# Row statistics and the scaling of k on GpSimd in a retention, SoLU and cosine-gate kernel

## The chip, the cores and the metric

The kernel runs on one core of one Trainium2 chip. The metric is device time in microseconds (us), the median of several runs. Five engines matter: PE (TensorE matmul; its weight loads have a row of their own, PEld), DVE (VectorE), ACT (ScalarE), POOL (GpSimd) and SP (SyncE, which here only issues DMAs). Each runs its own list of instructions in order: an instruction that waits holds up everything behind it on its engine.

## The reference

Three stages follow each other. Stage 1 is linear attention with decay, for 4 batches, 8 heads, 768 positions and head size 64. Stage 2 is a SoLU block with a normalisation, for 3072 rows. Stage 3 is a block with a cosine gate.

```python
for t in range(S):
    state = gamma * state + einsum('bhd,bhe->bhde', k[:, :, t], v[:, :, t])
    y[:, :, t] = scale * einsum('bhd,bhde->bhe', q[:, :, t], state)
...
h = x @ w_in                       # 3072x512 by 512x1024
sm = exp(h - max(h)); sm = sm / (sum(sm) + 1e-9)
solu = h * sm
ln = (solu - mean(solu)) / sqrt(var(solu) + 1e-6) * g_ln
x = ln @ w_out                     # 1024x512
...
h = x @ w_in                       # 512x2048
return (h * cos(h)) @ w_out        # 2048x512
```

## The kernel before

The work is cut into 24 attention steps of 64 positions for two batches, 24 row blocks of 128 rows for stage 2, and 6 blocks of 512 rows for stage 3. Matmuls keep fp32 accuracy by splitting each factor into a high and a low part (`split`: ACT rounds, DVE subtracts) and multiplying three of the four pairs. The weights arrive as 64-bit floats and are taken apart in `load_w`: one ACT instruction (L158) and four on DVE (L161, L162, L164, L167).

An attention step n has these parts:

- `load_step` issues six DMAs from SP: `kt` (L91), two halves of `X` (q, L93 and L94), two halves of `W` (v, L96 and L97), `kn` (k by rows, L98). The buffers go round: 3 for X, kn and W, 2 for kt and mg.
- `att_prep` multiplies the mask by the step's decay (`mg`, L219, one POOL instruction of 128x512) and scales `kn` by a constant per partition and pair of heads (L223, four ACT instructions of 128x128).
- `score_pair` and `state_pair` are the PE parts (L230, L231 and L241); `score_mask` (DVE, L248) writes the masked scores into X; `state_copy` (ACT, L255 and L256) copies the running state into W of the next step; `att_out` (PE L287, DVE L290) gives the rows x.

Stage 2 of a row block n: `split_x` (L125 on ACT, L128 on DVE), `mm1` (PE L315) in two column halves, then `norm`. `norm` is a chain over ACT, DVE and POOL: DVE takes the maximum (L323), ACT the exponential with its sum (L324), DVE the product with h and its sum (L325); then come the one-column statistics `sm` (128x1): minus the mean (L327, DVE), the square of the deviations (L328, ACT, result `junk`), the sum of exponentials plus 1e-9 (L329, DVE), its square times 1e-6 (L330, DVE), the variance plus that (L332, DVE), the power -1/2 (L334, POOL), and mean times that power (L335, DVE). L336 (ACT) applies scale and bias to `u`. Two row blocks later in program order `transp` transposes u on PE (L351), splits it (`lth` on ACT L354, `ltl` on DVE L355), and `mm2` multiplies (PE L368); its result goes to DRAM through ACT (`ys`, L372). `load_o1` prepares the weights of mm2 (L180 on ACT, L181 on DVE). Weights for stage 3 are unpacked between these steps and parked in DRAM (L191). Stage 3 (`up`, `down`) uses PE L393 and L418 and none of the lines above.

The order on PE is the order of the program, as written by hand at the end of `body`. The other engines' orders are made by the scheduler, which may move an instruction ahead of earlier ones. So `kn` of a step can be scaled, in ACT's order, well before the step itself.

Of the kernel before, what the change touches and what calls it, by code (L numbers as in the profile page):

```python
# [15 lines left out]
AF = mybir.ActivationFunctionType  # L16
ALU = mybir.AluOpType
# [4 lines left out]
B, H, S, D = 4, 8, 768, 64  # L22
# [3 lines left out]
NHP = H // 2  # L26
DM = H * D
FF1 = 1024
# [22 lines left out]
def body(ctx: ExitStack, tc: tile.TileContext, qx, kt, kn, vn, c_sc, c_mg,  # L51
         w_in1, w_out1, gln, w_in2, w_out2, out):
    nc = tc.nc
# [52 lines left out]
    cs = const.tile([128, 3, NI, NHP], F32, name="cs")  # L106
# [109 lines left out]
    def att_prep(n):  # L216
        bp, i = steps[n]
        d = st[n]
        nc.gpsimd.tensor_tensor(out=d["mg"], in0=mg, in1=cs[:, 0:2, i].unsqueeze(3).to_broadcast([128, 2, NHP, C]),  # L219
                                op=ALU.mult)  # L220
        if i + 1 < NI:
            for a in range(NHP):
                nc.scalar.activation(out=d["kn"][:, a], in_=d["kn"][:, a], func=AF.Copy, scale=cs[:, 2, i, a:a + 1])  # L223

    def score_pair(n, j):
        d = st[n]
# [91 lines left out]
    def norm(n):  # L318
        h = hs.pop(n)
        sm = sms[n % 3]  # L320
        junk = moe.tile([128, 2, 512], BF16, tag="junk", name="junk")
        u = p_u.tile([128, 2, 512], F32, tag="u", name="u")
        nc.vector.tensor_reduce(out=sm[:, 0:1], in_=h, axis=AX.XY, op=ALU.max, negate=True)  # L323
        nc.scalar.activation(out=u, in_=h, func=AF.Exp, bias=sm[:, 0:1], accum_out=sm[:, 1:2])  # L324
        nc.vector.scalar_tensor_tensor(out=u, in0=u, scalar=1.0, in1=h, op0=ALU.mult, op1=ALU.mult,  # L325
                                       accum_out=sm[:, 2:3])
        nc.vector.tensor_scalar(out=sm[:, 3:4], in0=sm[:, 2:3], scalar1=-1.0 / FF1, scalar2=None, op0=ALU.mult)  # L327
        nc.scalar.activation(out=junk, in_=u, func=AF.Square, bias=sm[:, 3:4], accum_out=sm[:, 4:5])  # L328
        nc.vector.tensor_scalar(out=sm[:, 5:6], in0=sm[:, 1:2], scalar1=1e-9, scalar2=None, op0=ALU.add)  # L329
        nc.vector.scalar_tensor_tensor(out=sm[:, 6:7], in0=sm[:, 5:6], scalar=1e-6, in1=sm[:, 5:6],  # L330
                                       op0=ALU.mult, op1=ALU.mult)
        nc.vector.scalar_tensor_tensor(out=sm[:, 7:8], in0=sm[:, 4:5], scalar=1.0 / FF1, in1=sm[:, 6:7],  # L332
                                       op0=ALU.mult, op1=ALU.add)
        nc.gpsimd.tensor_tensor(out=sm[:, 8:9], in0=sm[:, 7:8], in1=mhalf, op=ALU.pow)  # L334
        nc.vector.tensor_tensor(out=sm[:, 9:10], in0=sm[:, 3:4], in1=sm[:, 8:9], op=ALU.mult)  # L335
        nc.scalar.activation(out=u, in_=u, func=AF.Identity, scale=sm[:, 8:9], bias=sm[:, 9:10])  # L336
        lns[n] = u

# [118 lines left out]
    def attend():  # L457
        n = nxt[0]
        if n >= ns:
            return  # L460
        nxt[0] += 1
        if 4 < n + 2 < ns:
            load_step(n + 2)
        if n == 0:
            att_state(n)
            att_out(n)
        if n + 1 < ns:
            att_prep(n + 1)
            if n > 0 and "lt" in p2:
                att_both(n)  # L470
            else:
                att_scores(n + 1)
        if n > 0:
            if "lt" not in p2:
                att_state(n)
            att_out(n)
        if n == ns - 1:
            att.close()
            p2["psh"] = ctx.enter_context(tc.tile_pool(name="psh", bufs=3, side="right", space=PSUM, reuse_waits="tile"))
            p2["sb"] = ctx.enter_context(tc.tile_pool(name="sb2", bufs=1, side="right", reuse_waits="tile"))  # L480

    def first(n, c):
        if c == 1 and 0 < n < 2 * NG - 1:
            split_x(n + 1)
        mm1(n, c)
        if c == 1:
            norm(n)
# [5 lines left out]
    load_step(2)  # L493
    fetch_w1(1)
    att_prep(0)
    att_scores(0)
    weights(KD)
    att_state(0)
    att_out(0)
    att_prep(1)  # L500
    att_scores(1)
    split_x(0)
# [164 lines left out]
```

## Time and profile before

| | |
|---|---|
| time, median of 3 runs | 931.45 us (930.01 to 932.88) |
| span of the profiled execution | 932.8 us; no other time of its own is given, and the highest run, 932.88, is nearest |
| PE busy | 893.4 us, 96% |
| PEld busy | 765.1 us, 82% |
| DVE busy | 622.7 us, 67% |
| ACT busy | 455.5 us, 49% |
| POOL busy | 48.0 us, 5%, 60 instructions |
| mean granted TensorE clock | 0.985 of full speed |
| DMA | 85.28 MB, mean 91 GB/s |

Busy time is the time in which an engine executes; shares are of the span. A row with `[... <-X]` or "idle before" says how long the engine stood idle before an instruction, and which instruction, transfer or engine ended that idle time. The chain of waits follows the end of the program back to its start, always to what released each piece. In order listings, `x4` means four such instructions in a row; numbers behind tile names (sm_121) tell buffers of one tile apart.

### The profile page before, as it was taken

To read this page: it belongs to the slowest core of one execution; us is meant where nothing else is said; L and a number is where in the kernel's file an instruction comes from. 1 tells how busy PE (TensorE), PEld (TensorE's weight loads), DVE (VectorE), ACT (ScalarE), POOL (GpSimd) and SP (SyncE) were. 2 spreads that over 40 slices of the span, in tenths; PEclk is the share of its full clock that TensorE was granted. 3 is DMA by queue.
4 is the path that set the end of the run, shared out by engine and by line. 5 is a ranking of instruction groups with operands and counts; after the bars stand their busy time and mean duration, and the time that the engine had idled before them with its cause. 6 is when DMAs were issued, how large, how long until landed. Compare 5 with 4: busy or idle time off the path is not lost.

```text
span 932.8 us, 16044 instructions
## 1 busy us (share of the span) xinstructions
PE 893.4 (96%) x6464; PEld 765.1 (82%) x6464; DVE 622.7 (67%) x1090; ACT 455.5 (49%) x768; POOL 48.0 (5%) x60
## 2 busy tenths in 40 slices
PE   4787999989899999999999999999999999999997
PEld 4676889879799989998888888888888888888886
DVE  6899887587667754566766655756575665656654
ACT  4677666556656555554534333433443343344332
POOL 2112100101011000000000000000000000000000
PEclk7999899989999999999999999999999999999999
DMA  9986354565547422133012002000300030001001
GB/s 260 313 252 194 106 158 146 184 204 161 188 131 226 157 93 90 64 108 111 24 35 56 1 1 73 19 0 1 91 1 1 7 84 1 1 24 45 1 1 46
DMA packets 41884, 85.28 MB, mean 91 GB/s; under 512 B 5457, under 2 KB 11729, under 8 KB 41809
## 3 DMA queue, kind: packets, MB, share of 16 engines
q1 hardware_dynamic: 41376, 83.91, 30.0%
q8 instruction: 51, 0.84, 0.4%
q10 hardware_dynamic: 432, 0.34, 0.1%
q14 instruction: 25, 0.20, 0.1%
HBM read 64.30 MB, written 19.92 MB: 90 GB/s over the span
## 4 chain that ended last, share of the span: by engine, by line
PE 84%; DVE 6%; DMA 5%; ACT 2%; issue 2%; SPq 1%; POOL 0%; DVEq 0%; ACTq 0%
PE h L393 28%; PE acc L418 28%; PE y L368 13%; PE h L315 10%; DMA kn<-kn_dram 3%; PE tr L351 2%; PE y L287 2%; DMA W<-vn_dram 1%; PE sc L230 1%; DVE X L248 1%; DVE wt L164 1%; DVE wt L161 1%; ACT kn L223 1%; ACT junk L328 1%; DVE wt L162 0%
## 5 line engine op out<-in xcount | busy, mean ns | idle before, releaser
L393 PE MATMUL h<-yh,w2h 128*128 128x512 f32 x384 | 149.6, 390 | 0.0
L393 PE MATMUL h<-yl,w2h 128*128 128x512 f32 x384 | 149.4, 389 | 0.0
L393 PE MATMUL h<-yh,w2l 128*128 128x512 f32 x384 | 149.4, 389 | 0.0
L418 PE MATMUL acc<-o2h,gh 128*128 128x512 f32 x384 | 149.4, 389 | 0.0
L418 PE MATMUL acc<-o2h,gl 128*128 128x512 f32 x384 | 149.4, 389 | 0.0
L418 PE MATMUL acc<-o2l,gh 128*128 128x512 f32 x384 | 149.4, 389 | 0.0
L404 ACT ACTIVATE r<-r,hp 128x512 f32<-128x512 f32 x96 | 69.5, 724 | 144.5 <-DVE r L403 144.5
L368 PE MATMUL y<-lth,o1h 128*128 128x256 f32 x384 | 110.2, 287 | 0.0
L368 PE MATMUL y<-ltl,o1h 128*128 128x256 f32 x384 | 108.8, 283 | 0.0
L368 PE MATMUL y<-lth,o1l 128*128 128x256 f32 x384 | 108.6, 283 | 0.0
L401 DVE SCALAR_TENSOR_TENSOR r<-ki,h 128x512 f32<-128x512 int32 x96 | 66.0, 687 | 62.9 <-ACT ki L400 61.9
L405 DVE TENSOR_TENSOR r<-r,h 128x512 f32<-128x512 f32 x96 | 66.0, 687 | 61.6 <-ACT r L404 61.6
L128 DVE TENSOR_TENSOR gl<-r,gh 128x512 fp32r<-128x512 f32 x96 | 66.3, 691 | 45.9 <-ACT gh L125 45.4
L400 ACT ACTIVATE ki<-h 128x512 int32<-128x512 f32 x96 | 57.3, 597 | 74.7 <-PE h L393 74.1
L125 ACT ACTIVATE gh<-r 128x512 fp32r<-128x512 f32 x96 | 60.7, 632 | 65.4 <-DVE r L405 65.4
L393 PEld LDWEIGHTS h<-yh,w2h 128*128 128x128 f32 x384 | 72.1, 188 | 14.9
L418 PEld LDWEIGHTS acc<-o2h,gl 128*128 128x128 f32 x384 | 72.1, 188 | 15.0
L393 PEld LDWEIGHTS h<-yl,w2h 128*128 128x128 f32 x384 | 72.1, 188 | 15.0
L418 PEld LDWEIGHTS acc<-o2l,gh 128*128 128x128 f32 x384 | 72.1, 188 | 14.9
L418 PEld LDWEIGHTS acc<-o2h,gh 128*128 128x128 f32 x384 | 72.0, 188 | 14.9
L393 PEld LDWEIGHTS h<-yh,w2l 128*128 128x128 f32 x384 | 72.1, 188 | 14.8
L315 PE MATMUL h<-w1h,xh 128*128 128x512 f32 x192 | 77.9, 406 | 0.0
(77 smaller groups left out, 1554.3 us busy)
## 6 DMA issues: line engine op xcount, KB each, us to landing
raw<-w_in_dram SPq DMA_DIRECT2D x24, 512.0 KB, 4.4
raw<-w_out_dram SPq DMA_DIRECT2D x24, 512.0 KB, 4.8
kt<-kt_dram SPq DMA_DIRECT2D x24, 256.0 KB, 4.9
X<-qx_dram SPq DMA_DIRECT2D x48, 128.0 KB, 5.0
W<-vn_dram SPq DMA_DIRECT2D x48, 128.0 KB, 4.6
kn<-kn_dram SPq DMA_DIRECT2D x24, 256.0 KB, 5.1
y1d<-ys SPq DMA_DIRECT2D x24, 256.0 KB, 2.1
yt<-y1d SPq DMA_DIRECT2D x24, 256.0 KB, 2.9
```

The source lines that it names most:

```text
L125: op = nc.scalar.activation(out=hi, in_=src if head is None else head, func=AF.Copy)
L128: nc.vector.tensor_tensor(out=lo, in0=src, in1=hi.bitcast(F32), op=ALU.subtract)
L287: nc.tensor.matmul(out=y[64 * par:64 * par + 64, j], lhsT=d["W"][:, par, j], rhs=d["X"][:, par, j], start=True, stop=True)
L315: nc.tensor.matmul(out=h[:, c], lhsT=a[:, k], rhs=w[:, k, cs], start=(k + m == 0), stop=(k == KD - 1 and m == 2))
L351: nc.tensor.transpose(out=tr[:, e, t * 128:(t + 1) * 128], in_=lns[2 * g + t].rearrange("p c f -> p (c f)")[:, j * 128:(j + 1) * 128], ide ...
L368: nc.tensor.matmul(out=y1[:, e], lhsT=w[:, j, ds], rhs=a[:, j % 2], start=(m == 0), stop=(m == 3 * K1 - 1))
L393: nc.tensor.matmul(out=h, lhsT=w[:, k, cs], rhs=a[:, k], start=(m == 0), stop=(m == 3 * KD - 1))
L400: nc.scalar.activation(out=ki, in_=h, func=AF.Identity, scale=INV2PI, bias=0.25)
L401: nc.vector.scalar_tensor_tensor(out=r, in0=ki, scalar=-C1, in1=h, op0=ALU.mult, op1=ALU.add)
L404: nc.scalar.activation(out=r, in_=r, func=AF.Sin, bias=hp[:, 0:1])
L405: nc.vector.tensor_tensor(out=r, in0=r, in1=h, op=ALU.mult)
L418: nc.tensor.matmul(out=acc, lhsT=a[:, ts_], rhs=w, start=(j == 0 and m == 0), stop=(j == K2 - 1 and m == 2))
```

## The change

Two edits. In `att_prep` one POOL instruction over 128x512 scales kn, with the constants broadcast along the 128 columns of a pair of heads, in place of four ACT instructions over 128x128. In `norm` the instructions of L329, L330, L332 and L335 go from DVE to POOL, with forms that POOL has (the factor 1e-3 is applied before squaring, so the square is 1e-6 times as before); L327, minus the mean, stays on DVE.

```diff
@@ att_prep
         if i + 1 < NI:
-            for a in range(NHP):
-                nc.scalar.activation(out=d["kn"][:, a], in_=d["kn"][:, a], func=AF.Copy, scale=cs[:, 2, i, a:a + 1])
+            nc.gpsimd.tensor_tensor(out=d["kn"], in0=d["kn"], in1=cs[:, 2, i].unsqueeze(2).to_broadcast([128, NHP, 2 * D]),
+                                    op=ALU.mult)
@@ norm
-        nc.vector.tensor_scalar(out=sm[:, 5:6], in0=sm[:, 1:2], scalar1=1e-9, scalar2=None, op0=ALU.add)
-        nc.vector.scalar_tensor_tensor(out=sm[:, 6:7], in0=sm[:, 5:6], scalar=1e-6, in1=sm[:, 5:6],
-                                       op0=ALU.mult, op1=ALU.mult)
-        nc.vector.scalar_tensor_tensor(out=sm[:, 7:8], in0=sm[:, 4:5], scalar=1.0 / FF1, in1=sm[:, 6:7],
-                                       op0=ALU.mult, op1=ALU.add)
+        nc.gpsimd.tensor_scalar(out=sm[:, 5:6], in0=sm[:, 1:2], scalar1=1e-9, scalar2=1e-3,
+                                op0=ALU.add, op1=ALU.mult)
+        nc.gpsimd.tensor_tensor(out=sm[:, 6:7], in0=sm[:, 5:6], in1=sm[:, 5:6], op=ALU.mult)
+        nc.gpsimd.tensor_scalar(out=sm[:, 7:8], in0=sm[:, 4:5], scalar1=1.0 / FF1, scalar2=sm[:, 6:7],
+                                op0=ALU.mult, op1=ALU.add)
         nc.gpsimd.tensor_tensor(out=sm[:, 8:9], in0=sm[:, 7:8], in1=mhalf, op=ALU.pow)
-        nc.vector.tensor_tensor(out=sm[:, 9:10], in0=sm[:, 3:4], in1=sm[:, 8:9], op=ALU.mult)
+        nc.gpsimd.tensor_tensor(out=sm[:, 9:10], in0=sm[:, 3:4], in1=sm[:, 8:9], op=ALU.mult)
```

In the changed kernel the square is L331; the other line numbers are as before, but for kn's scaling, which is L222. PE's order is the same instruction for instruction, SP's the same but for a handful of neighbours that change places. Of POOL's 22 new kn instructions and 96 new statistics, the place matters.

ACT, near the start of the program, after the first unpacked weights (`xh` is the split of the first row block). Before, kn of steps 1 and 2 stands ahead of the state copies and of a weight's high part:

```order
L125 ACTIVATE xh<-x_265 128x512
L223 ACTIVATE kn<-kn,cs 128x128 x4
L125 ACTIVATE w1h<-wt 128x512
L223 ACTIVATE kn<-kn,cs 128x128 x4
L255 ACTIVATE W<-S 64x512
L256 ACTIVATE W<-S 64x512
L125 ACTIVATE w1h<-wt 128x512
```

and in the changed kernel:

```order
L125 ACTIVATE xh<-x_262 128x512
L125 ACTIVATE w1h<-wt 128x512 x2
L255 ACTIVATE W<-S 64x512
L256 ACTIVATE W<-S 64x512
```

Both weight parts now follow xh directly.

ACT, at the tenth row block (its statistics are in sm_121), before:

```order
L324 ACTIVATE u,sm_121<-h,sm_121 128x1024
L255 ACTIVATE W<-S 64x512
L256 ACTIVATE W<-S 64x512
L223 ACTIVATE kn<-kn,cs 128x128 x4
L328 ACTIVATE junk,sm_121<-u,sm_121 128x1024
L336 ACTIVATE u<-u,sm_121 128x1024
L158 ACTIVATE wt<-raw 128x512
```

and in the changed kernel:

```order
L324 ACTIVATE u,sm_121<-h,sm_121 128x1024
L255 ACTIVATE W<-S 64x512
L256 ACTIVATE W<-S 64x512
L328 ACTIVATE junk,sm_121<-u,sm_121 128x1024
L336 ACTIVATE u<-u,sm_121 128x1024
L158 ACTIVATE wt<-raw 128x512
```

kn is gone from ahead of junk; u and the unpacking of a weight still stand in the same order behind it.

POOL, at the same tenth row block, as a piece of the difference (- before, + changed):

```order
+L329 TENSOR_SCALAR sm_121<-sm_121 128x1
+L331 TENSOR_TENSOR sm_121<-sm_121 128x1
+L222 TENSOR_TENSOR kn<-kn,cs 128x512
 L219 TENSOR_TENSOR mg<-mg,cs 128x512
+L332 TENSOR_SCALAR sm_121<-sm_121 128x1
 L334 TENSOR_TENSOR sm_121<-sm_121,mhalf 128x1
+L335 TENSOR_TENSOR sm_121<-sm_121 128x1
```

The scaling of kn, and mg behind it, now stand on POOL between the first and the second half of the row block's statistics.

## Rows read from the trace of the kernel before

**Rows 1.** Busy time by stretch: us from:to and length, then each engine, PEclk, DMA
```profile
27.00:41.00 14.00, 9.07 (x113) 7.29 (x112) 13.86 (x25) 8.76 (x19) 2.45 (x2) 0.88 1.06 295
41.00:93.50 52.50, 42.60 (x759) 35.50 (x757) 50.79 (x91) 40.10 (x78) 10.80 (x11) 0.99 0.80 230
93.50:256.00 162.50, 154.80 (x1677) 138.56 (x1678) 120.17 (x239) 99.34 (x175) 18.52 (x20) 0.96 0.53 163
256.00:380.00 124.00, 124.00 (x1172) 113.15 (x1171) 80.41 (x168) 68.77 (x113) 11.13 (x14) 1.00 0.42 133
```

**Rows 2.** Who waited for whom, PE: us in total, times, longest us
```profile
PE tr L351 <- DVE ltl L355: 7.6, 5, 4.1
...
PE tr L351 <- DVE sm L329: 3.8, 1, 3.8
```

**Rows 3.** The chain of waits through the tenth row block: start us, us, what
```profile
173.33 7.86 DMA kn<-kn_dram
...
181.22 1.28 ACT kn L223 x4
182.50 1.14 ACT junk L328 x2
...
183.90 0.56 POOL sm L334
...
184.74 0.04 ACT u L336
...
190.65 0.61 DVE ltl L355
```

**Rows 4.** Groups of ACT instructions, 27 to 93.5 us: count, busy us, mean ns, idle before
```profile
L223 ACT ACTIVATE kn<-kn,cs 128x128 f32<-128x128 f32 x36 | 11.6, 392 | 4.9 <-DMA kn<-kn_dram 4.9
```

**Rows 5.** Groups of POOL instructions, whole program
```profile
L219 POOL TENSOR_TENSOR mg<-mg,cs 128x512 f32<-128x512 f32 x24 | 27.2, 1137 | 210.1 <-DVE x L290 162.0 <-DVE sm L330 45.2 <-DMA cs<-c_sc_dram 2.4
L334 POOL TENSOR_TENSOR sm<-sm,mhalf 128x1 f32<-128x1 f32 x24 | 17.8, 743 | 119.9 <-DVE sm L332 119.9
...
L112 POOL MEMSET mhalf<- 128x1 f32 x1 | 0.1, 93 | 0.0
```

**Rows 6.** DVE and POOL in order of time, 54 to 57 us
```profile
54.15 0.69 DVE L167 SCALAR_TENSOR_TENSOR raw<-raw,wt 128x512 int32<-128x512 int32 x1
...
55.70 1.09 POOL L219 TENSOR_TENSOR mg<-mg,cs 128x512 f32<-128x512 f32 x1 [0.46 <-DVE x L290]
55.81 1.53 DVE L167 SCALAR_TENSOR_TENSOR raw<-raw,wt 128x512 int32<-128x512 int32 x1
```

**Rows 7.** Groups of DVE instructions, 27 to 93.5 us
```profile
L248 DVE TENSOR_TENSOR X<-sc,mg 64x512 f32<-64x512 f32 x18 | 12.3, 684 | 0.2
L167 DVE SCALAR_TENSOR_TENSOR raw<-raw,wt 128x512 int32<-128x512 int32 x11 | 10.1, 919 | 0.1
...
L161 DVE TENSOR_SCALAR wt<-wt 128x512 f32<-128x512 f32 x11 | 6.2, 572 | 0.0
L290 DVE TENSOR_TENSOR x<-y,mg 128x512 f32<-128x512 f32 x9 | 6.2, 689 | 0.2
L162 DVE TENSOR_SCALAR wt<-wt 128x512 int32<-128x512 int32 x11 | 5.3, 497 | 0.0
L325 DVE SCALAR_TENSOR_TENSOR u<-u,h 128x1024 f32<-128x1024 f32 x4 | 4.9, 1218 | 0.1
L323 DVE TENSOR_REDUCE sm<-h 128x1 f32<-128x1024 f32 x4 | 4.9, 1214 | 1.2 <-PE h L315 1.2
...
L335 DVE TENSOR_TENSOR sm<-sm 128x1 f32<-128x1 f32 x3 | 1.3, 432 | 0.0
```

**Rows 8.** DVE in order of time, single instructions
```profile
10.18 0.43 DVE L161 TENSOR_SCALAR wt<-wt 128x512 f32<-128x512 f32 x1 [0.77 <-ACT wt L158]
...
26.63 0.69 DVE L128 TENSOR_TENSOR w1l<-raw,w1h 128x512 fp32r<-128x512 f32 x1 [2.98 <-ACT w1h L125]
...
49.45 0.14 DVE L327 TENSOR_SCALAR sm<-sm 128x1 f32<-128x1 f32 x1
49.52 0.15 DVE L330 SCALAR_TENSOR_TENSOR sm<-sm 128x1 f32<-128x1 f32 x1
49.58 0.42 DVE L161 TENSOR_SCALAR wt<-wt 128x512 f32<-128x512 f32 x1
```

**Rows 9.** ACT in order of time, 19 to 24 us
```profile
19.74 1.28 ACT L223 ACTIVATE kn<-kn,cs 128x128 f32<-128x128 f32 x4 [3.40 <-DMA kn<-kn_dram]
...
23.57 1.28 ACT L223 ACTIVATE kn<-kn,cs 128x128 f32<-128x128 f32 x4 [2.03 <-DMA kn<-kn_dram]
```

## The prediction before the run

> **What bounds the kernel now.** I read the table of busy time by stretch first, since the page's 96% for PE is a mean over stages with different limits. From 256 us to the end PE never stands still [rows 1]; what the change touches there is hidden, and stage 3 does not contain it at all. Between 41 and 93.5 us it is otherwise: DVE is busy 50.79 of 52.5 us, and PE only 42.60; between 27 and 41 us DVE is busy 13.86 of 14. DVE's in-order list sets the pace there. That stretch ends when PE's first transpose is released, which waited 3.8 us for DVE [rows 2]; a DVE that arrives there later shifts everything behind it by the same amount. In the third stretch, 93.5 to 256 us, PE is short of the full 162.5 us by 7.7 us, and the waits of PE name the reason: transposes waited five times, 7.6 us in all, for `ltl` [rows 2]. These are three places, at the sixth, tenth and fourteenth row block.
>
> The chain of waits through the tenth block says where such a wait comes from [rows 3]. The transfer of kn lands at 181.2 us; ACT, which has stood at kn's first instruction, scales it (1.28), makes junk (1.14), then a statistic on DVE, the power on POOL (0.56), one more on DVE, and u begins on ACT at 184.74. Behind u stand two weights' unpacking and, at the end, ltl at 190.65. So the price of kn standing ahead of junk on ACT is the late landing, and the path from landing to u is 3.5 us.
>
> **The change, part by part.**
>
> *kn on POOL: what it does to DVE.* Of the 22 scalings, 36 ACT instructions or 9 scalings lie between 27 and 93.5 us [rows 4], where DVE sets the pace. Each becomes one POOL instruction of mg's shape and kind, and mg takes 1.09 us undisturbed (its mean is 1.137) [rows 5, 6]. POOL has the time. But mg already shows a price: an L167 that took 0.69 us took 1.53 when it began just after mg, and ended with it plus its own work [rows 6]; a loss of 0.84. In the groups of that stretch [rows 7] the same can be added up. Eleven L167 cost 10.1 us where 11 times 0.69 is 7.6, a loss of 2.5; eleven L161 cost 6.2 where 11 times 0.43 [rows 8] is 4.7, a loss of 1.5; eleven L162 5.3 where the same shape gives 4.7, 0.6; three L335 1.3 where 0.15 each (as L330's in [rows 8]) is 0.45, 0.85. That is 5.4 us for the eight mg of the stretch, 0.68 each. Instructions that read PSUM show no such loss: eighteen L248 at a mean of 684 ns, nine L290 at 689, and the long L325 and L323. They are 28.3 of the stretch's 66.5 us, 43%. mg is released by the end of L290 and so nearly always meets an unpacking instruction; kn is released by a DMA and comes anywhere. With 57% at 0.84 and 43% at about half the loss, since a PSUM instruction covers only part of 1.09 us, a scaling costs DVE 0.6 to 0.65. I take 0.6, nearest to mg's own mean. **9 times 0.6 is +5.4 us.** The ends are 0, if every scaling falls on DVE instructions that it does not hold, and 9 times 0.84, 7.6.
>
> The Trainium skill has this as a rule (SBUF — State Buffer, "Who interferes with whom"): DVE and GpSimd share a pair of SBUF ports that is locked for a whole instruction, against DVE instructions in a two-port mode or with two SBUF inputs; whoever starts first blocks the other fully. The rows on L167 agree; by the rule alone, every scaling at the full 1.09, the term would be 9.8 us.
>
> *Statistics on POOL: what it does to DVE.* Twelve DVE instructions (four for each of the first three row blocks) vanish ahead of the first transpose. They are not worth their 0.15 us: consecutive ones begin 0.07 apart [rows 8], so this gives 0.8 back. Their long cases (L335 above) are mg's lock, which the next instruction would meet instead. In return twelve small POOL instructions may hold DVE. Their cost is not in the trace; the nearest rows are a fill of one column at 0.093 us and the power at 0.55 to 0.56 [rows 3, 5]. I take 0.1, since mg's 512 columns at 1.09 us leave little for a fixed cost and the power is the one dear function; half of them meeting a DVE instruction costs 0.6. **Together 0**, with ends at -0.8 (no lock) and +5.9 (twelve locks of 0.56 less 0.8).
>
> *kn off ACT, at the start.* DVE stood still 2.98 us for a weight's high part [rows 8] that ACT could not make while it waited 2.03 us for kn and scaled it for 1.28 [rows 9]. In the new order both high parts follow xh directly. DVE could be 3 us earlier. Not all of it stays: the first state products must now wait for one whole POOL instruction of 1.09 us where PE could start on the first of four pieces of 0.39, the next weights arrive from a DMA system that is full (share 1.06 between 27 and 41 us [rows 1]), and DVE waits 1.2 us for PE's h before the first L323 [rows 7]. I take half, **-1.5**, with ends at 0 and -3.0.
>
> *The three waits of PE.* kn leaves ACT, but the piece of POOL's order for the tenth block has kn, and mg behind it, ahead of L332. So POOL now stands where ACT stood. From the landing: kn 1.09, mg 1.09, L332 0.1, the power 0.56, L335 0.1, and a hop of about 0.07 between any two: 3.2 us where it was 3.5. Behind u ACT's order is unchanged: the next weight, ys, a weight, lth. I take 0.35 off each of the three, **-1.1**; the ends are -7.6, when the waits vanish, and +1.5, 0.5 for each if the small instructions cost nearer to the power.
>
> *Rest.* Off POOL's new waits hang two others. mg behind kn now ends about 183.4 (181.2 and twice 1.09), and DVE's score mask of the next step needs it; DVE reaches that only behind ltl, at 190.65 [rows 3], 7 us later. The state products of that step come later still. ACT's freed 34 us (88 times 0.39 [rows 4]) lie beside a PE that does not wait for ACT in [rows 2] except through the three places above. Both at nothing; if those 7 us of cover went, each step's score mask would wait for POOL's 2.2 us.
>
> Sum: +5.4 + 0 - 1.5 - 1.1 = +2.8 us. The profiled execution has a span of 932.8, 1.35 above the median of the three runs shown; added to its span the sum gives 935.6, added to the median **934.2 us**. A difference of 0.3%, 2.8 us, is about what a measurement of this kernel can tell from no change, so the forecast lies just on that line.
>
> **The rivals.**
>
> *The waits dissolve (faster).* If POOL reaches L332 before it has to stand at kn, because the landing comes earlier against the row block than it does now, then the three waits of PE go: -7.6 in place of -1.1, and the sum is -3.7: 927.7 us. It decides where kn lands before junk's end, 3.7 us earlier than at the tenth block now. For it: DVE no longer stands at L332, and SP's queue waits for DVE's unpacked weights. Against it: kn's transfer is issued at 173.33 us, as soon as PE has let its buffer go, takes 7.86 us, and none of this is changed.
>
> *The lock at its full price (clearly slower).* If kn holds DVE at mg's rate nearly every time, 7.6, if the small instructions lock for a third of the power's time, +1.5, and nothing of the 3 us at the start survives, the sum is 7.6 + 1.5 - 1.1 = +8.0: 939.5 us. The rows on mg speak for it, the share of PSUM readers against it. This is also where the Trainium skill's rule on the ports, read strictly, points.
>
> *Nothing.* If the scalings fall mostly on PSUM readers (0.3 each, +2.7) and the gains come as counted (-1.5 and -1.1), the time is 931.5. For it: the arrival of a DMA has no tie to DVE's unpacking.
>
> **How the numbers follow.** The forecast with its neighbourhood, 930 to 937 us, 0.42: it splits evenly around the line, 0.21 same and 0.21 slower. The waits dissolve, wholly or in part, 0.25: 0.22 faster, 0.03 same. The full lock 0.19, all slower. Nothing 0.14, 0.13 same and 0.01 faster. Sums: faster 0.23, same 0.37, slower 0.40. The range reaches to the first rival and beyond it by less than a microsecond, 927, and to the full lock, 940; left out are the two together with a better start, and a lock by the small instructions near its upper end, each about 1 in 10. The likeliest case's own range is 930 to 937.
>
> **What would show it.** In the changed profile: L167, L161 and L162 between 27 and 93.5 us longer in total by about 5 us; POOL's kn near 1.09 us, or up to 0.69 more where DVE had begun first; the first transpose 3 to 5 us later; waits of tr for ltl still there, 6 to 7 us. Wrong would be: unpacking instructions no longer than now (then the lock is no matter for kn), a first transpose that is earlier than 93.5 us, or waits of tr below 3 us in all.

## The result and the profile after

The changed kernel takes 939.46 us, the median of four runs (937.42 to 940.24), beside 930.73 us for the kernel before on the same chip: ratio 1.0086, 95% interval [1.0061, 1.0110]. It is slower by 8.7 us by the medians, where 2.8 was forecast. The time lies inside the range, near its upper end.

One warning ahead of the profiles. The profiled execution of the kernel before has a span of 932.8 us, near the top of its runs, and that of the changed kernel (935.2) stands for 937.42, the fastest of its four. Read against each other they show 2.4 of the 8.7 us. Both kernels were therefore profiled once more in the experiments: 928.8 and 936.7 us. Where the two pairs disagree, both numbers are given.

The stretches of [rows 1], for the changed kernel (columns: from:to, length, then PE, PEld, DVE, ACT, POOL, PEclk, DMA share, GB/s):

```profile
27.00:41.00 14.00, 11.65 (x148) 9.13 (x147) 13.82 (x23) 5.48 (x10) 4.54 (x4) 0.88 1.04 294
41.00:93.50 52.50, 44.10 (x760) 36.98 (x758) 49.46 (x77) 31.85 (x50) 23.48 (x33) 0.97 0.78 232
93.50:256.00 162.50, 153.92 (x1667) 136.62 (x1668) 117.80 (x196) 89.43 (x142) 38.12 (x72) 0.97 0.53 162
256.00:380.00 124.00, 123.38 (x1165) 112.08 (x1164) 76.71 (x129) 64.49 (x102) 21.08 (x51) 1.00 0.42 134
```

DVE is no busier between 27 and 93.5 us than it was, which already speaks against the step that was meant to cost most. In the third stretch PE is busy 153.92 us where it was 154.80, although ACT and DVE have less to do. And in the fourth, PE no longer runs without a gap.

What PE waited for, the counterparts of the two lines of [rows 2] and one that is new:

```profile
PE tr L351 <- DVE ltl L355: 6.5, 9, 2.2
PE tr L351 <- DVE u L325: 5.4, 1, 5.4
...
PE h L315 <- DVE u L325: 1.2, 2, 0.7
```

The transposes still wait for ltl, nine times where it was five, 6.5 us in all where it was 7.6; the second profiles have 6.5 us and, for the kernel before, 5.2. The groups of POOL instructions beside [rows 5], whole program (busy us, mean ns, idle before and what ended it):

```profile
L219 POOL TENSOR_TENSOR mg<-mg,cs 128x512 f32<-128x512 f32 x24 | 27.8, 1159 | 33.2 <-DVE x L290 26.1 <-DVE sm L327 4.6 <-DMA cs<-c_sc_dram 2.5
L222 POOL TENSOR_TENSOR kn<-kn,cs 128x512 f32<-128x512 f32 x22 | 24.9, 1134 | 56.9 <-DMA kn<-kn_dram 47.0 <-PE y L368 9.8
L334 POOL TENSOR_TENSOR sm<-sm,mhalf 128x1 f32<-128x1 f32 x24 | 15.4, 642 | 2.0
L332 POOL TENSOR_SCALAR sm<-sm 128x1 f32<-128x1 f32 x24 | 9.7, 403 | 26.7 <-ACT junk L328 26.7
L329 POOL TENSOR_SCALAR sm<-sm 128x1 f32<-128x1 f32 x24 | 6.0, 248 | 162.3 <-ACT u L324 162.3
L335 POOL TENSOR_TENSOR sm<-sm 128x1 f32<-128x1 f32 x24 | 5.8, 241 | 1.9
L331 POOL TENSOR_TENSOR sm<-sm 128x1 f32<-128x1 f32 x24 | 4.6, 193 | 2.0
```

kn and mg cost what mg had shown. The one-column statistics cost 0.19 to 0.40 us on the mean, not 0.1. And POOL stands 47.0 us at kn for its transfer.

The tenth row block again, as [rows 3] had it before. POOL in order of time (start us, length, then what it is, and in brackets the idle time before it):

```profile
176.31 0.19 POOL L329 TENSOR_SCALAR sm<-sm 128x1 f32<-128x1 f32 x1 [5.11 <-ACT u L324]
176.59 0.19 POOL L331 TENSOR_TENSOR sm<-sm 128x1 f32<-128x1 f32 x1
180.41 1.04 POOL L222 TENSOR_TENSOR kn<-kn,cs 128x512 f32<-128x512 f32 x1 [3.64 <-DMA kn<-kn_dram]
181.41 1.04 POOL L219 TENSOR_TENSOR mg<-mg,cs 128x512 f32<-128x512 f32 x1
182.44 0.27 POOL L332 TENSOR_SCALAR sm<-sm 128x1 f32<-128x1 f32 x1
182.78 0.55 POOL L334 TENSOR_TENSOR sm<-sm,mhalf 128x1 f32<-128x1 f32 x1
183.41 0.19 POOL L335 TENSOR_TENSOR sm<-sm 128x1 f32<-128x1 f32 x1
```

and the chain of waits through the next block, which in the kernel before had no transfer of kn on it:

```profile
192.42 6.97 DMA kn<-kn_dram
...
199.56 0.96 issue
200.52 1.04 POOL mg L219
...
201.90 0.56 POOL sm L334
```

POOL is idle for 3.64 us, then does kn, mg and the rest of the statistics one behind the other. ACT's u starts at 183.63. From the landing, at 180.28, to u are 3.35 us, where the kernel before had 3.5. The wait at the head of the line moved from ACT to POOL, and it is on the chain more often: between 93 and 300 us the chain of the kernel before has three transfers of kn on it, in both profiles, that of the change four, that of its second profile five. It is not that POOL stands at more transfers: ACT in the kernel before stood at nine in that stretch, 24.4 us in all (second profile: eight, 19.3), POOL in the change at seven, 28.4 us (nine, 36.8).

**A yardstick for all runs.** PE's list is the same in all kernels timed here. Two of its instructions cut the time into three: the first transpose, and the first matmul of `acc` in stage 3. From `acc` to the end of the span it is 516.4 to 516.5 us in every profile below, so nothing there moved. The second column gives DVE's busy time up to the first transpose, the third the time between the two instructions.

| kernel (one profile each) | first transpose, us | DVE busy until then | to first `acc` |
|---|---|---|---|
| before; again | 93.5; 93.4 | 79.59; 79.60 (140 instr.) | 323.0; 319.0 |
| statistics alone; again | 94.7; 93.3 | 78.40; 78.86 (128) | 316.2; 317.6 |
| kn alone | 95.8 | 83.18 (140) | 321.2 |
| change; again | 94.8; 96.8 | 80.86; 83.32 (128) | 324.0; 323.6 |
| kn on POOL for steps 0 to 10 | 96.6 | 81.57 (128) | 320.3 |
| kn on POOL from step 11 | 96.6 | 81.05 (128) | 321.9 |
| change, kn held in order | 98.6 | 82.94 (128) | 315.1 |
| mg twice, no kn | 97.5 | 85.51 (128) | 314.8 |
| no kn at all | 96.1 | 78.13 (128) | 311.5 |

The middle stretch tells most of the story: 315 us where POOL has all its work but does not stand at kn's transfer, 321 to 324 where it does, 316 to 318 with the statistics on POOL and kn on ACT. It is no clean measure, though. The kernel before has 323.0 in one profile and 319.0 in the other. The columns also depend on each other: the two profiles of the statistics alone reach `acc` at the same 410.9 us, with starts 1.4 us apart. The kernel with kn on POOL for steps 0 to 10 does not stand at kn there and still has 320.3; its profiled execution, 935.2 us, is the slowest of its twelve, whose median is 932.79.

What fills the middle stretch is not waiting alone. The change, and then the change with kn held in order (columns as above):

```profile
94.80:418.83 324.03, 316.12 (x3109) 285.13 (x3110) 215.90 (x354) 176.09 (x276) 59.43 (x125) 0.99 0.46 144
98.57:413.71 315.14, 312.53 (x3108) 283.49 (x3109) 219.33 (x354) 176.24 (x276) 64.01 (x127) 1.00 0.46 148
```

Of the 8.9 us between them 5.3 are idle time of PE (7.9 against 2.6), and 3.6 are busy time for the same list. PE's clock goes with that: it stood at half of full speed (1.2 of 2.4 GHz) for 8.7 us of the change's stretch and 2.8 us of the other. One such time in the change came right behind a wait of 2.24 us:

```profile
250.31:253.72 3.41, 3.25 (x56) 2.52 (x60) 3.41 (x6) 1.77 (x3) 0.00 (x0) 0.50 0.92 299
```

In the kernel before the half clock lasted 12.5 us in one profile and 6.8 in the other, and PE was busy 315.3 and 313.7 us. With kn on POOL for steps 0 to 10 it was 11.2 us, with PE busy 315.7 and idle only 4.6. That these falls of the clock are a consequence of the waits is not shown here; a wait that is removed may give back more than its own length.

### The profile page after: what moved, and what is told of

The parts are those of the page before. It is cut to its first block, busy times and chain, and to the rows that moved or that the text cites. A ratio compares the mean times of both kernels' runs of the same rounds, so it can differ in the third digit from the quotient of the medians.

```text
span 935.2 us, 16027 instructions
## 1 busy us (share of the span) xinstructions
PE 897.6 (96%) x6464; PEld 767.1 (82%) x6464; DVE 616.4 (66%) x994; ACT 428.8 (46%) x680; POOL 96.2 (10%) x178
## 4 chain that ended last, share of the span: by engine, by line
PE 79%; DVE 7%; DMA 6%; issue 3%; POOL 2%; ACT 2%; SPq 1%; POOLq 0%; DVEq 0%; ACTq 0%
PE h L393 28%; PE acc L418 28%; PE y L368 11%; PE h L315 8%; DMA kn<-kn_dram 3%; PE tr L351 2%; PE y L287 1%; PE sc L230 1%; DVE wt L164 1%; DVE X L248 1%; DMA X<-qx_dram 1%; DVE wt L161 1%; POOL mg L219 1%; DMA raw<-w_in_dram 1%; DVE wt L162 1%
## 5 line engine op out<-in xcount | busy, mean ns | idle before, releaser
L315 PE MATMUL h<-w1h,xh 128*128 128x512 f32 x192 | 78.4, 409 | 1.2 <-DVE u L325 1.2
```

The lines of the kernel that those rows point to most:

```text
L315: nc.tensor.matmul(out=h[:, c], lhsT=a[:, k], rhs=w[:, k, cs], start=(k + m == 0), stop=(k == KD - 1 and m == 2))
```

## The experiments

Two theories were tested. By the **port theory** kn on POOL stretches DVE's unpacking at the start. By the **queue theory** kn's wait for its transfer stands in POOL's list ahead of mg and the statistics, and u and the transposes come late all through stage 2. The expectations below, written before each run, also call the first the lock theory and the second the chain theory. A third, the occupancy theory, says that POOL's time itself costs, wherever it stands.

**Both kernels again.** No edit.

> The kernel before, unchanged, as a run of its own, for a second profile of it. Both theories: within 0.3% (2.8 us) of before, and PE's waits of transposes for ltl at three places again, 6 to 9 us in all.

> The changed kernel once more, for a second profile and a narrower interval. Both theories: 5 to 10 us above before. Lock theory (kn on POOL holds DVE at the start): the first transpose starts 3 us or more later than before's 93.5 us, and the difference at the end is about that of the first transpose. Chain theory (the row statistics now queue on POOL behind kn and mg, so u comes later and transposes wait): the first transpose within 2 us of before's, and PE's waits for ltl and for DVE's u between 100 and 300 us longer in total than before's 7.6 us by 4 us or more.

Measured: before 930.53 us, ratio 0.9991 [0.9971, 1.0012]; change 938.11 us, 1.0066 [1.0038, 1.0095]. The loss is there again, a little smaller. Against each other the second profiles put 3.3 us of it ahead of the first transpose and 4.6 behind it. Neither set of signs came whole. The first transpose was as late as the port theory asked for, but that is less than half of the loss; PE's waits for ltl and u behind it were 7.7 us (6.5 and 1.2), not 4 longer than 7.6. The second profile of the kernel before has 5.2 us of the ltl waits, below the 6 to 9 expected, so the 7.6 of its first was a high one.

**Each half alone.** kn on POOL with the statistics on DVE, and the reverse:

```diff
 kn alone (norm as before)
-            for a in range(NHP):
-                nc.scalar.activation(out=d["kn"][:, a], in_=d["kn"][:, a], func=AF.Copy, scale=cs[:, 2, i, a:a + 1])
+            nc.gpsimd.tensor_tensor(out=d["kn"], in0=d["kn"], in1=cs[:, 2, i].unsqueeze(2).to_broadcast([128, NHP, 2 * D]),
+                                    op=ALU.mult)
 statistics alone (att_prep as before)
-        nc.vector.tensor_scalar(out=sm[:, 5:6], in0=sm[:, 1:2], scalar1=1e-9, scalar2=None, op0=ALU.add)
+        nc.gpsimd.tensor_scalar(out=sm[:, 5:6], in0=sm[:, 1:2], scalar1=1e-9, scalar2=1e-3,
+                                op0=ALU.add, op1=ALU.mult)
...
```

> kn on POOL as in the changed kernel, statistics on DVE as before. Lock theory: nearly all of the loss, +6 to +9 us over before. Chain theory: kn still stands ahead of the power on POOL, but the other four statistics do not queue there, so +1 to +4 us.

> Statistics on POOL as in the changed kernel, kn in four ACT instructions as before. Lock theory: -1 to +2 us. Chain theory, if the statistics alone are too slow on POOL: +4 to +8 us; if they are slow only behind kn: -1 to +2 us, and then kn_only is small as well.

> The statistics alone on GpSimd, kn on ScalarE, a second time, to settle whether that half by itself beats the kernel before: ratio of the first time 0.9981, so 927 to 931 us; by either theory it stands 6 to 9 us below the change.

Measured: kn alone 935.09 us, ratio 1.0055 [1.0033, 1.0077]; the statistics alone 929.43 us, 0.9981 [0.9963, 1.0000], and in a later run beside other kernels 931.18 us, 1.0013 [0.9995, 1.0031]. The statistics change nothing that can be measured; the loss, or most of it, belongs to kn. At about 4 us by the medians and 5.1 by the ratio, kn alone lies at the upper end of what the chain theory named (1 to 4) or above it, and below what the lock theory named (6 to 9). The first time the statistics alone looked like a small gain, which the second did not bear out.

**Where in the program.** The change, with kn on POOL for the first 11 steps only, as shown, or with `n >= 11` for the others only (the rest on ACT):

```diff
-            nc.gpsimd.tensor_tensor(out=d["kn"], in0=d["kn"], in1=cs[:, 2, i].unsqueeze(2).to_broadcast([128, NHP, 2 * D]),
-                                    op=ALU.mult)
+            if n < 11:
+                nc.gpsimd.tensor_tensor(out=d["kn"], in0=d["kn"], in1=cs[:, 2, i].unsqueeze(2).to_broadcast([128, NHP, 2 * D]),
+                                        op=ALU.mult)
+            else:
+                for a in range(NHP):
+                    nc.scalar.activation(out=d["kn"][:, a], in_=d["kn"][:, a], func=AF.Copy, scale=cs[:, 2, i, a:a + 1])
```

> The change, with kn scaled on GpSimd only for attention steps 0 to 10 and by four ScalarE instructions from step 11 on (statistics on GpSimd throughout). Ten kn of GpSimd still lie beside the packed splits of 27 to 93.5 us. Port theory (the loss is made at the start, where GpSimd's kn stretches VectorE's work): near the change, 936 to 939 us, and first transpose at 95 to 97 us. Queue theory (kn's wait for its transfer stands in GpSimd's list ahead of the statistics, and u and the transposes come late, from 93 us on): from the first transpose to the end 832 to 835 us as in the run with the statistics alone, so 930 to 933 us in all, ScalarE's waits for sm ahead of u (L336) back from 29 to about 11 us between 93 and 300 us.

> The reverse: kn by ScalarE for steps 0 to 10, on GpSimd from step 11 on, statistics on GpSimd. Port theory: the start is that of the statistics alone, so 929 to 931 us. Queue theory: most of the change's loss stays, 934 to 938 us, with the first transpose at about 94.5 us and over 20 us of ScalarE waiting for sm ahead of u between 93 and 300 us.

Measured: early 932.79 us, 1.0021 [0.9999, 1.0043]; late 935.93 us, 1.0049 [1.0026, 1.0072]. As the queue theory said, by the time and by ACT: its wait for the statistics ahead of u, 93 to 300 us, was 10.1 us in the first and 29.0 in the second, and 29.2 in the change. By the medians the larger part of the loss is made by the steps from 11 on, most of whose scalings lie behind the first transpose; the two intervals overlap. Two signs of the early kernel missed: its first transpose, 96.6 us, was where the port theory had it (95 to 97), and from there to the end its profile, the slowest run, has 836.8 us, not 832 to 835. The late kernel's first transpose, 96.6 us, did not come as forecast (94.5): PE there waited 12.7 us for two transfers of X at the very start, where it was 9.0 to 11.0 in the kernel before and the change, and one kn that was moved up to 93.57 us held an o1l of DVE (below). A start moves by up to 2 us from run to run (the change: 94.8 and 96.8), so a single profile's first transpose carries little.

**kn one turn later, held there.** From step 4 on, kn of step n is scaled at the head of its own turn, and the scheduler may not move it; on POOL, as shown, and with the four instructions on ACT:

```diff
+    def kn_scale(n):
...
+            op = nc.gpsimd.tensor_tensor(out=d["kn"], in0=d["kn"], in1=cs[:, 2, i].unsqueeze(2).to_broadcast([128, NHP, 2 * D]),
+                                    op=ALU.mult)
+            if n > 3:
+                tc.keep_in_program_order(op)
...
         if n + 1 < ns:
+            if n > 3:
+                kn_scale(n)
             att_prep(n + 1)
```

> The change, with kn of step n (from step 4 on) scaled in step n's own turn, one turn later, and held in the order of the program, so that its transfer landed long before and GpSimd's list does not wait for it ahead of the statistics. As many GpSimd instructions as in the change. Queue theory: GpSimd's wait for kn's transfer falls from 28 to 37 us (93 to 300 us) to under 10, ScalarE's wait for sm ahead of u from 29 to under 18, and the time from 938 to 930 to 934 us. Port theory or a plain slower-engine theory (the instructions themselves cost, wherever they stand): 937 to 940 us. A third outcome is that the state matmuls now wait for kn: then TensorE shows S waiting for kn by over 1 us a step after 93 us.

> Statistics on GpSimd, kn on ScalarE as in the kernel before, but from step 4 on in step n's own turn and held in the order of the program. ScalarE's 18 us of waiting for kn's transfer (93 to 300 us) should go. Queue theory for ScalarE's own list: 926 to 929 us, under the 929.4 of the statistics alone. If waits on ScalarE lie off the path there: 929 to 931 us; if holding the order costs more than the wait: over 931 us.

Measured: 1064.64 us, 1.1439 [1.1401, 1.1477], and 1000.03 us, 1.0740 [1.0705, 1.0775]. Both miss by far, and it is the third outcome, much larger than thought. PE's waits with POOL:

```profile
PE S L249 <- POOL kn L220: 118.7, 16, 13.7
```

and with ACT:

```profile
PE S L249 <- ACT kn L221: 67.9, 18, 9.6
```

At that place kn stands, in the engine's list, behind instructions of the row block ahead, which need PE's h, and PE's next state products need kn: the lists wait for each other in turn. On POOL, for one, kn begins at 253.26 us, directly behind the last statistic at 253.12, and POOL had stood 13.56 us for ACT's exponential ahead of these statistics. As a test of the queue theory this one says nothing, since a larger wait took the place of the one removed.

**Taking the wait away, not the work.** In the first kernel POOL multiplies mg a second time where kn stood; in the second the lines of kn are gone. Both leave out the scaling, so their state is made from unscaled k.

```diff
         if i + 1 < NI:
-            nc.gpsimd.tensor_tensor(out=d["kn"], in0=d["kn"], in1=cs[:, 2, i].unsqueeze(2).to_broadcast([128, NHP, 2 * D]),
-                                    op=ALU.mult)
+            nc.gpsimd.tensor_tensor(out=d["mg"], in0=mg, in1=cs[:, 0:2, i].unsqueeze(3).to_broadcast([128, 2, NHP, C]),
+                                    op=ALU.mult)
```

> The change, with the scaling of kn left out and in its place on GpSimd a second copy of the same step's multiplication of mg (same size, beside the first, no operand that a transfer brings), so that GpSimd runs as many instructions of the same lengths at nearly the same places but never waits for kn's transfer. The state is made from unscaled k. Queue theory (the wait for the transfer is what costs): 928 to 932 us, GpSimd's wait for kn gone, ScalarE's wait for sm ahead of u under 18 us between 93 and 300 us. Occupancy theory (a GpSimd microsecond in front of the statistics, or the shared port, costs by itself): 935 to 939 us.

> The change, with the scaling of kn left out on every engine (the state is made from unscaled k). What is left is the statistics on GpSimd with neither ScalarE's four instructions nor GpSimd's one. Floor for both: 925 to 929 us if ScalarE's kn in the kernel with the statistics alone costs something on the path, 929 to 931 us if it costs nothing. The difference of the run with mg twice to this one is the price of GpSimd's occupancy: under 2 us by the queue theory, over 5 us by the occupancy theory.

Measured: mg twice 932.15 us, 1.0021 [1.0010, 1.0032]; no kn 922.85 us, 0.9925 [0.9906, 0.9944]. Neither theory holds alone. With as much POOL work but no transfer to wait for, 6.0 to 7.3 of the change's microseconds are gone; that is the queue. (These runs were made on different chips; by the ratios, each to the kernel before on its own chip, it is 4.2 to 6.0.) The time fell to the upper end of what the queue theory named, but its sign on ACT missed: the wait ahead of u was 23.0 us, not under 18.

What is left, 932.15 less 922.85, both on one chip, is 9.3 us, over the 5 that the occupancy theory asked for, and the kernel without kn is faster than either of its forecasts. So the scalings of k together cost some microseconds also where POOL does not stand at their transfer: the two runs with the statistics on POOL and kn on ACT (929.43 and 931.18) lie 6.6 and 8.3 above the kernel without it, 5.2 and 8.2 by the ratios. Part of it with mg twice is the hold on DVE, which is busy 7.4 us longer up to the first transpose (85.51 against 78.13). The profiles of these two kernels differ by only 4.7 us of span: the one is the fastest run of its kernel (930.64), the other (926.09) the slowest of its own.

**The same instructions, kn behind mg.** The change, with kn's instruction held at its place in the program:

```diff
-            nc.gpsimd.tensor_tensor(out=d["kn"], in0=d["kn"], in1=cs[:, 2, i].unsqueeze(2).to_broadcast([128, NHP, 2 * D]),
-                                    op=ALU.mult)
+            op = nc.gpsimd.tensor_tensor(out=d["kn"], in0=d["kn"],
+                                         in1=cs[:, 2, i].unsqueeze(2).to_broadcast([128, NHP, 2 * D]), op=ALU.mult)
+            tc.keep_in_program_order(op)
```

What this does to POOL's list, at the step that has no kn of its own (the last of the first two batches) and the one behind it; in the change:

```
L222 TENSOR_TENSOR kn<-kn,cs 128x512
L219 TENSOR_TENSOR mg<-mg,cs 128x512
L332 TENSOR_SCALAR sm_121<-sm_121 128x1
L334 TENSOR_TENSOR sm_121<-sm_121,mhalf 128x1
L335 TENSOR_TENSOR sm_121<-sm_121 128x1
L329 TENSOR_SCALAR sm_122<-sm_122 128x1
L331 TENSOR_TENSOR sm_122<-sm_122 128x1
L222 TENSOR_TENSOR kn<-kn,cs 128x512
L219 TENSOR_TENSOR mg<-mg,cs 128x512
```

and held in order (its lines behind 222 are one higher):

```
L219 TENSOR_TENSOR mg<-mg,cs 128x512
L333 TENSOR_SCALAR sm_121<-sm_121 128x1
L335 TENSOR_TENSOR sm_121<-sm_121,mhalf 128x1
L336 TENSOR_TENSOR sm_121<-sm_121 128x1
L330 TENSOR_SCALAR sm_122<-sm_122 128x1
L332 TENSOR_TENSOR sm_122<-sm_122 128x1
L219 TENSOR_TENSOR mg<-mg,cs 128x512
L222 TENSOR_TENSOR kn<-kn,cs 128x512
```

In the change the scheduler had moved kn one whole step ahead of mg, so from there on POOL asks for each kn as soon as its transfer is issued; held in order, kn stands behind mg of its own step, in every step from there on.

> The change, with kn's instruction held at its place in the order of the program, which puts it behind mg and sets one kn of the first rounds later in GpSimd's list. Queue theory: kn's transfer is waited for less (under 20 us between 93 and 300 us) and the time falls to 932 to 936 us; if holding it in place only moves the wait to the state matmuls, TensorE shows S waiting for kn and the time is 938 us or more.

Measured: 931.44 us, 1.0016 [1.0000, 1.0033]. The place of kn in POOL's list is worth 6.7 us against the change's second timing, with nothing removed; that was on another chip, and by the ratios it is 0.5%, 4.7 us. It fell below the expected range.

One thing beside POOL's list moved. With the new list the scheduler also put 14 of DVE's 994 instructions at other places; at the tenth and the fourteenth row block the two ltl now follow each other, where the change has an unpacking instruction (L164, 0.68 us) between them. Other kernels here speak against this order as the cause: that with kn alone has ltl behind ltl at both places, and 321.2 us in the middle stretch; the statistics alone have L164 between, and 316 to 318.

POOL at the tenth row block, with kn held:

```profile
177.87 0.19 POOL L330 TENSOR_SCALAR sm<-sm 128x1 f32<-128x1 f32 x1 [4.95 <-ACT u L325]
178.15 0.20 POOL L332 TENSOR_TENSOR sm<-sm 128x1 f32<-128x1 f32 x1
180.57 1.05 POOL L219 TENSOR_TENSOR mg<-mg,cs 128x512 f32<-128x512 f32 x1 [2.23 <-DVE sm L328]
181.57 1.04 POOL L222 TENSOR_TENSOR kn<-kn,cs 128x512 f32<-128x512 f32 x1
182.59 0.27 POOL L333 TENSOR_SCALAR sm<-sm 128x1 f32<-128x1 f32 x1
182.94 0.55 POOL L335 TENSOR_TENSOR sm<-sm,mhalf 128x1 f32<-128x1 f32 x1
183.57 0.19 POOL L336 TENSOR_TENSOR sm<-sm 128x1 f32<-128x1 f32 x1
```

mg is done while ACT still makes junk (180.58 to 181.83 us), and kn finds its data there. kn ends 0.8 us behind junk, and the statistics follow at once; in the change the first of them began 2.2 us behind junk (182.44 against 180.27). ACT's exponential of this block began 1.57 us later than in the change (176.58 against 175.01), and yet u begins only 0.16 us later (183.79 against 183.63). ACT and PE, in the change's second profile and with kn held; waits of ACT between 93 and 300 us, and of PE. The change:

```profile
ACT u L336 <- POOL sm L335: 29.5, 14, 5.1
...
PE tr L351 <- DVE ltl L355: 6.5, 8, 2.6
```

kn held in order:

```profile
ACT u L337 <- POOL sm L336: 22.6, 14, 3.1
...
PE tr L352 <- DVE ltl L356: 2.5, 6, 0.8
```

POOL's waits for kn's transfer, 36.8 us in nine there, are gone, and no transfer of kn is on the chain between 93 and 300 us. The state matmuls did not wait instead: their waits for kn (2.6 us, both at the start) are what the change had (3.1 and 2.3).

No kernel here with the scaling in it beats the one before: the statistics alone and the change with kn held both come out level with it. Only the kernel that leaves the scaling out is faster. Putting the factor of k into some other operation, so that no instruction of its own is needed, was not tried.

## Why the prediction was right and wrong

**What bounds the kernel** was read right. Nothing moved behind stage 2, the start and the ltl waits were the places, and the first transpose came 1.3 to 3.3 us later, where 3 to 5 were named. That the time lies in the range is in part luck: it is outside the 930 to 937 of the case held likeliest, and the upper end, 940, was set for a full lock that did not come.

**The lock of kn on DVE (+5.4): right in kind, too large.** The same 128 DVE instructions lie ahead of the first transpose in the change and with the statistics alone. DVE's busy time up to it, with the statistics alone:

```profile
0.00:94.70 94.70, 69.81 (x1100) 59.05 (x1101) 78.40 (x128) 62.12 (x126) 22.26 (x40) 0.87 0.84 252
```

in the change:

```profile
0.00:94.80 94.80, 69.96 (x1101) 58.76 (x1101) 80.86 (x128) 47.86 (x75) 36.79 (x53) 0.96 0.85 251
```

and in the change's second profile:

```profile
0.00:96.80 96.80, 70.26 (x1101) 59.30 (x1102) 83.32 (x128) 47.71 (x75) 38.31 (x53) 0.89 0.83 246
```

With the other profile of the statistics alone (78.86), the term is 2.0 to 4.9 us. kn alone against the kernel before, with the same 140 instructions, gives 3.6. It did not appear where the prediction looked. In the groups of [rows 7], as the changed kernel has them between 27 and 93.5 us,

```profile
L164 DVE SCALAR_TENSOR_TENSOR wt<-raw,wt 128x512 int32<-128x512 int32 x11 | 8.3, 760 | 0.1
L162 DVE TENSOR_SCALAR wt<-wt 128x512 int32<-128x512 int32 x11 | 7.7, 706 | 0.0
L167 DVE SCALAR_TENSOR_TENSOR raw<-raw,wt 128x512 int32<-128x512 int32 x11 | 7.4, 685 | 0.1
L181 DVE SCALAR_TENSOR_TENSOR o1l<-raw,gcol,o1h 128x512 fp32r<-128x512 f32 x7 | 6.7, 969 | 0.1
...
L161 DVE TENSOR_SCALAR wt<-wt 128x512 f32<-128x512 f32 x10 | 4.3, 430 | 0.6 <-ACT wt L158 0.6
```

L162 lost 2.4 more than before, but L167 2.7 and L161 1.9 less: these three together are 2.2 us shorter, or 1.8 if the one L161 that left the window is allowed for, and not 5 longer. That is one of the signs which the prediction named for being wrong; but the lock is there, in rows that it had left out. L164 and o1l (L181) go from 683 and 740 ns on the mean to 760 and 969. In the kernel before they had been

```profile
L164 DVE SCALAR_TENSOR_TENSOR wt<-raw,wt 128x512 int32<-128x512 int32 x11 | 7.5, 683 | 0.1
...
L181 DVE SCALAR_TENSOR_TENSOR o1l<-raw,gcol,o1h 128x512 fp32r<-128x512 f32 x6 | 4.4, 740 | 0.0
```

mg's own losses moved when its place did, and the estimate had kept them. Nor did its own working give 0.6 for a scaling: 57% at 0.84 and 43% at half of that is 0.66, 5.9 us in all. The rule of the Trainium skill (SBUF — State Buffer, "Who interferes with whom") that was weighed, taken at the full 1.09 for each kn, gave 9.8 us; the trace gives at most half. No run shows how much of kn's time met instructions that it does not hold.

**The statistics (0): right.** DVE is busy 0.7 to 1.2 us less up to the first transpose (79.59 and 79.60 against 78.40 and 78.86), where 0.8 was named, and that with one o1l more ahead of it; the time did not change. The small POOL instructions were put at 0.1 us and are 0.19 to 0.40. Alone they cost nothing, as POOL then reaches them without waiting at kn.

**kn off ACT at the start (-1.5): not there.** DVE's idle time up to the first transpose, the time less its busy time, was 13.9 and 13.8 us before and is 13.9 and 13.5 in the change. It is the upper end of that term, 0. (With kn alone it is 12.6, so there 1.2 us of the gain can be seen.)

**The three waits of PE (-1.1) is the step that failed.** The middle stretch should have become about a microsecond shorter, and is 324.0 and 323.6 us where it was 323.0 and 319.0. The waits of tr for ltl did come as named, 6.5 us in both profiles of the change where 6 to 7 were forecast; but the 7.6 they were counted down from was one profile's, and the second has 5.2. To them come 1.2 us of PE waiting for u (h, L315) in each profile of the change, which were not there before and for which the sum has no term, and the growth of PE's busy time in the stretch, 316.1 and 315.8 us where it was 315.3 and 313.7. The prediction had the right rows of POOL's order ahead of it: kn, and mg behind it, between the halves of the statistics. It then priced that piece at one block, from the landing of a transfer taken over from the kernel before, with the small instructions at 0.1 us, and found 0.35 us of gain. For that block it was not far off: 3.35 us from landing to u, where it said 3.2. Two things were missed. The scheduler had not only put kn ahead of mg but a whole step ahead, and transfers of kn came onto the chain at more blocks ([rows 3] had one; the change's chain has kn at 175.27 and, above, 192.42). And the same piece without that wait would have been worth a gain: with kn held in order, or mg in its place, the stretch is 315 us. The price of kn's place in the list, 4.7 to 6.7 us, is thus about as large as the largest term of the sum, and the prediction set what hangs on it, mg's lateness among it, at nothing. How much of the price is mg's lateness and how much that of the statistics no run separates.

**The rivals.** The full lock gave 939.5, which is the time measured, by another way: its lock of 7.6 us was at most 4.9. The waits dissolving (927.7) had the right place of decision, when POOL comes to L332 and whether it has to stand at kn ahead of it; it needs kn behind mg, as the run with kn held shows: waits of tr for ltl 2.5 us. Even then the start ate the gain, 98.6 us to the first transpose in its one profile, and why it came so late is open.

**Open.** How the 1.3 to 3.3 us at the start divide between the lock, the transfers and PE's clock. The kernel without any kn, with the least DVE work (78.13), had its first transpose at 96.1 us, later than the change's first profile, with 8.1 us of PE waiting for one transfer of X.

## What to carry to other kernels

A new instruction on an engine that is nearly idle is not free if it waits for a transfer: the engine takes its list in order, and what counts is what stands behind the wait. Before such a move, read in the new order how far ahead the scheduler puts the instruction, and hold it behind what others wait for; here that won back what the move had cost, and no more. But not as late as its own use, which here cost 134 us against the kernel before. And where the difference sought is under 1%, cut several executions of each kernel at the same two instructions before believing a difference of two profiles.

## What the runs showed of the hardware

An o1l on DVE that, by the profile, began ahead of kn was held all the same. In the kernel with kn on POOL from step 11, DVE

```profile
93.19 1.97 DVE L181 SCALAR_TENSOR_TENSOR o1l<-raw,gcol,o1h 128x512 fp32r<-128x512 f32 x1
```

and POOL

```profile
93.57 1.03 POOL L223 TENSOR_TENSOR kn<-kn,cs 128x512 f32<-128x512 f32 x1
```

The o1l took 1.97 us, where 0.75 is its time undisturbed (in the change, at 92.64 us), and it ended 0.56 us behind kn. It had begun 0.38 us earlier by the profile. In the change kn began 0.52 us behind the o1l, which was not held. A fill of W (L101) ran on POOL just ahead of kn in both, and did not hold the o1l of the change. In [rows 6] the instruction that was held had begun 0.11 us after mg. By the Trainium skill (SBUF — State Buffer, "Who interferes with whom") the one that issues first blocks the other; the row of the held o1l does not agree, as far as the profile dates the starts, and POOL's are rough.
